# A new written order of operations for attention and token/channel mixing, with one load made to wait for a turned block

## The chip, the cores and the metric

The kernel runs on one core of one Trainium2 chip. The metric is the device time of one execution in microseconds, here the median of three runs. PE is the matmul engine, PEld its weight loads, DVE the vector engine, ACT the scalar engine, POOL is GpSimd, and SP is the engine that only issues DMAs. Names with a q behind them (SPq) are an engine's issuing part.

## The reference, cut to what matters

Sliding-window attention with a linear distance bias gives x; a token mix and a channel mix with residuals follow.

```python
# q, k, v: (8 batches, 8 heads, 576 positions, 64)
scores = 1/sqrt(64) * q @ k.T - slope[h] * |i - j|      # only 0 <= i - j < 128
x = softmax(scores) @ v                                  # -> (8, 576, 512)
h = relu(x.T @ w_tok1) @ w_tok2                          # 576 -> 256 -> 576
u = x + h.T
out = u + relu(u @ w_ch1) @ w_ch2                        # 512 -> 1536 -> 512
```

## The kernel before

Batches are handled in pairs. The 576 positions of a batch are four blocks of 128 and a tail of 64; in a pair the blocks have the numbers 0 to 3 (even batch), 4 to 7 (odd batch) and 8 (both tails). The work of `side(b)` prepares batch b: loads of q, k and v (POOL, L596, from f32 in memory to bf16 on the chip), their turned form `qkT`, scores (PE, L791 and L837), exponentials (ACT, L806), masks (DVE, L816), the product with v (PE, L871), reciprocals and normalisation (L901, L904 on DVE or L909 on ACT), and the token mix (L933 to L976), which writes `ub`, u in bf16 (DVE, L994). u is then turned to `uT`, by PE in the first batches, from batch 3 on by a transposing DMA that SP issues (L1002). From the second pair on SP's DMAs also turn q and k (L743). `main(b)` is the channel mix of batch b: chunks of four wide matmuls (L1491), or in batches 3 to 7 seven half-size products for eight (`unit`, L1391, with differences `tt` of `uT` made on DVE, L1354, copies out of PSUM into `raw` and `ob` buffers by ACT, L1406, or DVE, L1407, and joins on DVE, L1415 and L1417), then the second layer in the same manner (L1668, sums on DVE L1516, results added at L1639), tails (L1534, L1579, L1586), and stores (L1651, L1595) from SP or, for batches 5 and 6, from POOL. While `main(b)` runs on PE, `side(b + 1)` runs between its matmuls.

All of these are operations of a planner, `Plan`. Each has a number, an engine, the operations that it depends on, and buffers in rings. Nothing is chosen when the kernel is built: `ORDER` lists all operations by number (base 36) in one sequence, and each engine runs those that are its own in that sequence. `ELSEWHERE` lists the operations that run on their second engine (ACT for DVE or the reverse), and `PLACES` gives the ring slot of each buffer in the order of first use. So these three tables fix every engine's order, and which earlier buffer's readers an operation waits for. Semaphores between engines follow from them.

POOL issues its loads in that order from one queue; a load waits until its buffer is free, and those behind it wait too. In addition one operation of POOL, `pd`, a copy of four elements of `uT` into an unused corner of `zero` (L1025), holds POOL until batch 4's four blocks of u are turned:

```python
HOLDS = {4: ("v", 3, 0)}
```

SP's queue holds stores, turns of qk and turns of u in the order of the table.

Of the kernel before, what the change touches and what calls it, by code (L numbers as in the profile page):

```python
# [70 lines left out]
class Plan:  # L71
# [60 lines left out]
    def follow(self):  # L132
# [5 lines left out]
        for x in ELSEWHERE.split():  # L138
            o = ops[number(x)]
            o.eng, o.cost, o.emit = o.other  # L140
        line = {e: [o for o in seq if o.eng == e] for e in ("PE", "ACT", "DVE", "POOL", "SP")}
        succ = {o: [] for o in ops}
        left = {o: len(o.deps) for o in ops}
# [16 lines left out]
        at = dict.fromkeys(line, 0)  # L160
# [123 lines left out]
    def emit(self, spin):  # L284
# [20 lines left out]
        for _, _, go in sorted(work, key=lambda w: w[:2]):  # L305
# [37 lines left out]
ORDER = ("h i 4z f j g 52 k d e 0 l 59 7 1 2 8 4v m 3 4 4x n 4w 9 4y o a 55 5 41 50 42 56 43 53 57 44 51 p 58 54 5c q "  # L343
# [44 lines left out]
ELSEWHERE = ("4w 4y 56 5m 63 6i 71 74 82 86 8a a1 a5 b4 b6 c1 c3 ct cz fb fo ft fw gh gj gn gp gr gt gv h7 j0 j2 jk jw ku "  # L388
             "l5 ls lu m0 n8 na of oo op oz qa qd qq qv qy sl t3 t6 th uc uf uh us vd vi vn wv y0 y2 z5 zx 10a 10f 125 12m "
             "12p 130 13n 13q 144 14e 14h 14w 154")  # L390
PLACES = ("000232243674016170016710104526473452324062714260014501022423400510303647106542202567210123732010446005172042"
          "362051274206715214600503123154312004710320646027513140700140215467140010640713055567102605442020611541127230"
          "025262104700230014425051403512010500312141045110243012320140672042576220135742000764034632027316250001410345"
          "032144211356403132100450246021001275130420276110007602714237320407630130523116201136100600423450014031202753"
          "010221310424602240716150473245124022651103414372613403103250016362440743151304001632203241351701025422040305"
          "000654201226422044020117553524030170503214160073144603151242005002361430470201452220764207205106323324401126"
          "21054020440646533020470006402521147105523572030164250114")
UNIT_LATE = False
SECOND_LATE = False
GATE = True  # L400
# [33 lines left out]
def kernel(  # L434
# [15 lines left out]
    nc = tc.nc  # L450
# [464 lines left out]
    def token_mix(b, rank):  # L915
# [13 lines left out]
        for j in range(NJ):  # L929
            turn_ = blocks[1:] + blocks[:1] if half and pr in PAIRED else blocks  # L930
            for c, blk in enumerate(turn_):
                def go(j=j, c=c, blk=blk):
                    pe_.matmul(t1[j]()[:, :], lhsT=W1[:, blk % NC, j * P : (j + 1) * P], rhs=xb()[:, blk, :],  # L933
                               start=c == 0, stop=False)
# [62 lines left out]
        for blk in blocks:  # L997
            if b >= FROM_U:
                def turn(blk=blk):
                    c = blk % NC  # L1000
                    to = uTt()[:, :, :] if blk == TAIL else uT()[:, :, c * P : (c + 1) * P]
                    nc.sync.dma_start_transpose(out=to, in_=ub()[:, blk, :])  # L1002

                turned.setdefault(b, []).append(plan.op(
                    "SP", 1200, turn, rank(0), part=(uTt if blk == TAIL else uT, blk), reads=[(ub, blk)], bus=1000))
                continue
            ut = bank()

# [752 lines left out]
```

## Time and profile before

| | |
|---|---|
| median of 3 runs | 274.56 us (272.98 to 274.78) |
| profiled execution, own time | 274.01 us |
| its span, first to last instruction | 272.1 us |
| busy in the span: PE, DVE, ACT, POOL | 263.2, 234.0, 159.5, 114.8 us |
| instructions of PE, DVE, ACT, POOL | 3033, 533, 306, 147 |
| DMA: moved, packets | 38.59 MB, 160338 |

The span is shorter than the execution's own time by 1.9 us, which lie before the first and behind the last instruction. Busy time of PE is the time in which at least one matmul is in flight; matmuls overlap, so a busy PE can still start them late. A "turn" is a transposing DMA. "Landing" is the time at which a DMA's data are there, "issue" that at which its engine sends it.

### The profile page before, as it was taken

To read this page: it belongs to the slowest core of one execution; us is meant where nothing else is said; L and a number is where in the kernel's file an instruction comes from. 1 tells how busy PE (TensorE), PEld (TensorE's weight loads), DVE (VectorE), ACT (ScalarE), POOL (GpSimd) and SP (SyncE) were. 2 spreads that over 40 slices of the span, in tenths; PEclk is the share of its full clock that TensorE was granted. 3 is DMA by queue.
4 is the path that set the end of the run, shared out by engine and by line. 5 is a ranking of instruction groups with operands and counts; after the bars stand their busy time and mean duration, and the time that the engine had idled before them with its cause. 6 is when DMAs were issued, how large, how long until landed. Compare 5 with 4: busy or idle time off the path is not lost.

```text
span 272.1 us, 7520 instructions
## 1 busy us (share of the span) xinstructions
PE 263.2 (97%) x3033; PEld 195.6 (72%) x3033; DVE 234.0 (86%) x533; ACT 159.5 (59%) x306; POOL 114.8 (42%) x147
## 2 busy tenths in 40 slices
PE   7989999999999999999999999999899989999994
PEld 5767565776686656588877876688776768588883
DVE  7886598983996799889999899999899989987992
ACT  6974787144963469229991299428881379413900
POOL 8987977640680866601680137400740410003000
PEclk9999999999999999999999999999999999999999
DMA  8999999999999999999999899979999430044006
GB/s 197 179 170 181 150 191 183 149 111 181 190 142 169 176 139 230 161 116 232 80 177 149 221 141 78 124 183 164 147 165 111 129 107 2 12 88 149 8 0 193
DMA packets 160338, 38.59 MB, mean 142 GB/s; under 512 B 146544, under 2 KB 159472, under 8 KB 160304
## 3 DMA queue, kind: packets, MB, share of 16 engines
q0 software_dynamic: 109968, 19.64, 90.3%
q1 hardware_dynamic: 49104, 17.70, 33.9%
q10 hardware_dynamic: 1232, 0.79, 1.0%
q8 instruction: 23, 0.38, 0.6%
q14 instruction: 11, 0.09, 0.1%
HBM read 35.85 MB, written 9.44 MB: 166 GB/s over the span
## 4 chain that ended last, share of the span: by engine, by line
PE 71%; DMA 11%; issue 7%; DVE 5%; POOL 4%; ACT 1%; SPq 0%; POOLq 0%; DVEq 0%
PE ps L1668 24%; PE ps L1391 11%; PE ps L1491 11%; PE ps L871 5%; PE ps L933 4%; PE ps L976 4%; PE ps L791 3%; DMA qk<-in_k_dram 3%; PE ps L1534 3%; PE ps L1579 3%; DMA v<-in_v_dram 2%; DMA qkT<-qk 2%; DMA W<-in_moe_w_tok_dram 2%; POOL qk L596 2%; DVE r L1415 2%
## 5 line engine op out<-in xcount | busy, mean ns | idle before, releaser
L806 ACT ACTIVATE pe<-ps 128x1024 bf16<-128x1024 f32 (+1 forms) x56 | 51.8, 971 | 15.8 <-PE ps L791 15.8
L596 POOL DMA_DIRECT2D qk<-in_k_dram x35 | 29.9, 868 | 52.2 <-DMA qkT<-qk 49.0
L596 POOL DMA_DIRECT2D v<-in_v_dram x36 | 30.9, 867 | 30.8 <-PE ps L871 29.9
L1668 PEld LDWEIGHTS <-r 128*128 128x128 bf16 x384 | 36.6, 98 | 8.0 <-issue 1.3
L596 POOL DMA_DIRECT2D qk<-in_q_dram x35 | 30.3, 875 | 11.4 <-DMA qkT<-qk 7.6
L816 DVE TENSOR_TENSOR pe<-pe,mask 128x1024 bf16<-128x1024 bf16 (+1 forms) x48 | 30.3, 647 | 3.4 <-ACT pe L806 3.2
L1491 PE MATMUL ps<-uT,WC 128*128 128x512 bf16 x132 | 32.0, 379 | 0.0
L1406 ACT COPY raw<-ps 128x512 f32<-128x512 f32 x32 | 19.0, 596 | 21.8 <-PE ps L1391 11.9
L1668 PEld LDWEIGHTS <-s 128*128 128x128 bf16 x288 | 27.7, 98 | 5.2 <-issue 0.4
L909 ACT ACTIVATE xb<-ps,rt 128x64 bf16<-128x64 f32 x80 | 18.3, 324 | 19.2 <-DVE rt L901 19.1
L1415 DVE TENSOR_TENSOR r<-ps,raw 128x512 bf16<-128x512 f32 x37 | 24.6, 679 | 1.8 <-PE ps L1391 1.7
L1391 PE MATMUL ps<-tt,WS 128*128 128x256 bf16 x180 | 25.9, 273 | 0.0
L1668 PE MATMUL ps<-WC,r 128*128 128x256 bf16 x192 | 25.7, 273 | 0.0
L1391 PEld LDWEIGHTS <-WS 128*128 128x128 bf16 x240 | 21.9, 98 | 4.9 <-issue 1.2
L871 PEld LDWEIGHTS <-pe 128*128 128x128 bf16 (+1 forms) x480 | 20.4, 99 | 6.5 <-issue 1.4
L1668 PE MATMUL ps<-WT,r 128*128 128x256 bf16 x192 | 24.7, 273 | 0.0
L1668 PE MATMUL ps<-WT,s 128*128 128x256 bf16 x192 | 24.1, 273 | 0.0
L871 PE MATMUL ps<-v,pe 128*128 128x65 bf16 (+1 forms) x480 | 23.0, 194 | 0.6 <-ACT pe L806 0.3
L994 DVE TENSOR_TENSOR ub<-ps,xb 128x512 bf16<-128x512 f32 x32 | 21.0, 683 | 2.9 <-PE ps L976 2.7
L1497 ACT ACTIVATE r<-ps 128x512 bf16<-128x512 f32 x26 | 15.1, 613 | 10.0 <-PE ps L1491 8.7
L1639 DVE TENSOR_TENSOR raw<-ps,ub 128x512 f32<-128x512 f32 x27 | 18.3, 683 | 2.1 <-PE ps L1668 2.1
L1491 PEld LDWEIGHTS <-WC 128*128 128x128 bf16 x132 | 11.6, 98 | 11.8 <-issue 0.2
(145 smaller groups left out, 519.1 us busy)
## 6 DMA issues: line engine op xcount, KB each, us to landing
out_dram<-raw SPq DMA_DIRECT2D x19, 256.0 KB, 2.6
qk<-in_q_dram POOLq DMA_DIRECT2D x30, 128.0 KB, 4.9
qk<-in_k_dram POOLq DMA_DIRECT2D x30, 128.0 KB, 4.9
v<-in_v_dram POOLq DMA_DIRECT2D x28, 128.0 KB, 5.6
WC<-in_moe_w_ch_dram POOLq DMA_DIRECT2D x8, 384.0 KB, 7.6
out_dram<-raw POOLq DMA_DIRECT2D x8, 256.0 KB, 2.8
out_dram<-ob SPq DMA_DIRECT2D x5, 256.0 KB, 2.6
v<-in_v_dram POOLq DMA_DIRECT2D x16, 64.0 KB, 4.8
```

The lines of the kernel that those rows point to most:

```text
L596: nc.gpsimd.dma_start(out=to()[p0 : p0 + n, :, :], in_=rows(src, b, s0, n))
L806: act_.activation(out=pb()[:, e, :, lo:, c0:c1_], in_=wide(e)[:, :, lo:, c0:c1_], func=ACT.Exp, scale=scale)
L816: dve_.tensor_tensor(out=o, in0=o, in1=heads(mk, es), op=ALU.mult)
L871: pe_.matmul(view(e)[a:z, i, :], lhsT=pb()[:, e, i, kind, a:z], rhs=vb()[:, HEADS[e][i], 0 : D + 1], start=start, stop=stop, skip_group_ch ...
L909: act_.activation(out=x4()[:, i, :], in_=view(e)[r0:r1_, i, 0:D], func=ACT.Copy, scale=rt()[r0:r1_, 0, i, :])
L994: plan.op("DVE", 690, lambda blk=blk, ht=ht, hs=hs: dve_.tensor_tensor(out=ub()[:, blk, :], in0=ht()[:, hs], in1=xb()[:, blk, :], op=ALU.a ...
L1391: pe_.matmul(bk()[:, c * HS : (c + 1) * HS], lhsT=l(c, cb), rhs=r(cb), start=new and c == 0 and cb == 0, stop=cb == 1, skip_group_check=True)
L1406: return plan.op("ACT", 600, lambda: act_.copy(out=e()[:, :], in_=bk()[:, :]), rk + UNIT_RANK, makes=e, uses=[bk], other=("DVE", 690, lamb ...
L1415: add = plan.op("DVE", 690, lambda: dve_.tensor_tensor(out=o(), in0=half_of(bk), in1=half_of(e), op=ALU.add), rk + UNIT_RANK, uses=[bk, e] ...
L1491: pe_.matmul(ct()[:, :], lhsT=WC1[:, cb, t * P : (t + 1) * P], rhs=uT()[:, cb, :], start=cb == 0, stop=cb == NCB - 1)
L1639: dve_.tensor_tensor(out=v, in0=bk().rearrange("p (c n) -> p c n", c=2), in1=src, op=ALU.add)
L1668: pe_.matmul(bk()[:, c * HN : (c + 1) * HN], lhsT=l(t, c), rhs=w(t), start=first, stop=g == 1 and t == HK - 1, skip_group_check=True)
```

## The change

`ORDER`, `ELSEWHERE` and `PLACES` are replaced by new tables of the same length and kind: the same 1528 operations, numbered alike, in another sequence, with another choice of engine for part of those that have two, and other buffer slots. From the start, PE, DVE, ACT and POOL keep their order for about 23 us. A new table, `WAITS`, has one entry, `30:pc`: operation `30`, POOL's load of v for block 4 of the third pair (batches 4 and 5), depends on `pc`, SP's turn of block 3 of u of batch 4. In POOL's order the load is preceded by a copy of one element of that block of `uT`.

```diff
         for x in ELSEWHERE.split():
             o = ops[number(x)]
             o.eng, o.cost, o.emit = o.other
+        for x in WAITS.split():
+            o, d = (ops[number(y)] for y in x.split(":"))
+            o.deps.add(d)
+            o.emit = lambda d=d, go=o.emit: (d.touch(), go())
...
-ORDER = ("h i 4z f j g 52 k d e 0 l 59 7 1 2 8 4v m 3 4 4x n 4w 9 4y o a 55 5 41 50 42 56 43 53 57 44 51 p 58 54 5c q "
...
-         "6w 13 6t 73 6r 6x 74 79 6u 14 6y 75 17 6z 76 7g 7a 7b 7h 70 77 7c 78 7d 9k 7i 71 7j 7k 7e 7r 9l 7f 9m 9p 9q "
...
+         "6w 13 6t 73 6r 6x 74 79 6u 14 6y 75 7g 6z 7a 7h 70 76 7b 7i 17 18 77 9k 7j 78 71 7c 9l 7d 9m 7k 9n 7s 7q 1a "
...
+WAITS = "30:pc"
...
+                def touch(blk=blk):
+                    at = 0 if blk == TAIL else blk % NC * P
+                    nc.gpsimd.tensor_copy(out=zero[0:1, 2 * P : 2 * P + 1],
+                                          in_=(uTt() if blk == TAIL else uT())[0:1, 0, at : at + 1])
+
                 turned.setdefault(b, []).append(plan.op(
                     "SP", 1200, turn, rank(0), part=(uTt if blk == TAIL else uT, blk), reads=[(ub, blk)], bus=1000))
+                turned[b][-1].touch = touch
```

Lines behind the insertions move: a line of before stands 5 lines further on behind the tables (L596 is L601), and 11 further on behind the token mix (L1651 is L1662). Three places of the new order follow; rows give line, operation, output and inputs with buffer numbers, and the output's shape.

POOL at the load that now waits, before. The load `30` is the row that writes `v1_73`; loads of `qk` bring q or k of one block, loads of `v` the values.

```order
L596 DMA v3_75<-in_v_dram 128x8x64
L596 DMA qk1_68<-in_q_dram 128x8x64
L596 DMA qk0_67<-in_q_dram 128x8x64
L596 DMA v1_73<-in_v_dram 128x8x64
L596 DMA qk0_67<-in_k_dram 128x8x64
L596 DMA qk3_70<-in_k_dram 128x8x64
L596 DMA qk4_71<-in_q_dram 128x8x64
L596 DMA v0_72<-in_v_dram 128x8x64
```

And POOL after, at the same load, which now writes `v3_75`:

```order
L601 DMA qk4_71<-in_k_dram 128x8x64
L601 DMA qk4_71<-in_q_dram 128x8x64
L601 DMA qk3_70<-in_q_dram 128x8x64
L1011 COPY zero_117<-uT1_99 1x1
L601 DMA v3_75<-in_v_dram 128x8x64
L601 DMA qk3_70<-in_k_dram 128x8x64
L601 DMA qk4_71<-in_q_dram 128x8x64
L601 DMA qk2_69<-in_k_dram 128x8x64
L601 DMA v1_73<-in_v_dram 128x8x64
L601 DMA v4_76<-in_v_dram 128x8x64
L601 DMA qk0_67<-in_k_dram 64x8x64
L1036 COPY zero_117<-uT1_99 1x4
```

The waiting copy stands ahead of the load; the loads of v for blocks 5 and 6 (`v1_73`, `v4_76`) stand behind it. Operation `pd` (the last row) comes 25 rows earlier than before, where it stood among the last stores. Among the turns of batch 4 that of block 3 is now the third of four, where it was the fourth.

SP behind the turns of batch 5's u, before. `uTt0_100` is the tail's turn; the row that writes `qkT0_77` turns the block whose scores PE runs next.

```order
L1002 DMA_TRANSPOSE uT1_99<-ub0_92 128x4x128 x4
L1651 DMA out_0_dram<-raw1_105 128x2x256
L743 DMA_TRANSPOSE qkT2_79<-qk1_68 128x8x128
L1651 DMA out_0_dram<-raw3_107 128x2x256
L743 DMA_TRANSPOSE qkT3_80<-qk2_69 128x8x128
L1002 DMA_TRANSPOSE uTt0_100<-ub0_92 128x4x128
L1651 DMA out_0_dram<-raw0_104 128x2x256
L743 DMA_TRANSPOSE qkT4_81<-qk3_70 128x8x128
L1651 DMA out_0_dram<-raw4_108 128x2x256
L743 DMA_TRANSPOSE qkT0_77<-qk0_67 128x8x128
```

SP after, at the same place; the same turn now writes `qkT1_78`:

```order
L1007 DMA_TRANSPOSE uT0_98<-ub1_93 128x4x128 x4
L748 DMA_TRANSPOSE qkT6_83<-qk3_70 128x8x128
L1662 DMA out_0_dram<-raw1_105 128x2x256
L1007 DMA_TRANSPOSE uTt0_100<-ub1_93 128x4x128
L748 DMA_TRANSPOSE qkT5_82<-qk1_68 128x8x128
L748 DMA_TRANSPOSE qkT1_78<-qk2_69 128x8x128
L1662 DMA out_0_dram<-ob0_109 128x2x256
L1662 DMA out_0_dram<-raw0_104 128x2x256
L1662 DMA out_0_dram<-raw3_107 128x2x256
L748 DMA_TRANSPOSE qkT4_81<-qk4_71 128x8x128
L748 DMA_TRANSPOSE qkT6_83<-qk0_67 128x8x128
```

That turn now stands ahead of three stores; of the other turns of this stretch one has gone far ahead, and two stand behind the stores.

POOL's stores of batch 5, before; `ob0_109` is the tail's result, in two halves.

```order
L1595 DMA out_0_dram<-ob0_109 64x512
L1651 DMA out_0_dram<-raw4_108 128x2x256
L1651 DMA out_0_dram<-raw0_104 128x2x256
L1595 DMA out_0_dram<-ob0_109 64x512
L1651 DMA out_0_dram<-raw2_106 128x2x256
L1025 COPY zero_117<-uT0_98 1x4
L1651 DMA out_0_dram<-raw3_107 128x2x256
```

After:

```order
L1606 DMA out_0_dram<-ob0_109 64x512 x2
L1662 DMA out_0_dram<-raw2_106 128x2x256
L1662 DMA out_0_dram<-raw0_104 128x2x256 x2
L1662 DMA out_0_dram<-raw4_108 128x2x256
L1662 DMA out_0_dram<-raw1_105 128x2x256
```

Both halves of the tail now go first. The copy of the product that PE waited behind (L1407 on DVE before, into `raw0_104`) runs on ACT after (into `raw2_106`), and the store that frees its buffer is the third one of the row in both.

More of the change, by code (lines that the diff above doesn't have):

```diff
@@ L345 @@
          "x 6v 5u 5r y 6j 5s 46 47 66 72 6k 5v z 6a 48 6b 10 6d 6l 6g 6e 6h 6f 67 6m 6c 68 6i 11 69 6n 6p 6o 12 6s 6q "
[42 rows of a table removed]
[L388 to L397, printed above, removed]
[42 rows of a table added]
+ELSEWHERE = ("4w 4y 56 5m 63 6i 71 74 78 7b 7f 84 86 88 ai b9 bz c1 c3 cd cj ct cx el fm ft gh gj gp gv gx hf jc ji jl ko "
+             "la ls n8 na oh op oz po pt qa qq qv qy sl t3 t6 u7 uc us vd vi vl wt y2 z8 zg zx 10f 10i 125 12p 13q 13v 140 "
+             "146 149 14b 14e 14h 154")
+PLACES = ("000122344672036170016710104526473452324062734260014501032423100140213475607220046272034001536024216272520001"
+          "067415233720651324602562032157301122443136002107460120531521315331011275000234004217304224465300240402164571"
+          "026203502273020350410523114514224041131020203041251251320240160240617542020615142061257243603201543101720214"
+          "405253711443150312004572021062027502027060276002721420673206540140710020232170022060032410473304456011053421"
+          "401341210462433124070326473012241152642201132213042746022301410106254025121703752003416504460221514200515144"
+          "750204201730416223110204006532135065132470316020131004031240452060540521120100471220761572205306322750021132"
+          "64100210704650611734500306212410753404174012530615235213")
+WAITS = "30:pc"
 UNIT_LATE = False
```

82 rows, old and new, of the table ORDER are left out of this document.

## The prediction

> **What bounds the kernel now.** First the page's part on busy time and its row of the granted clock.
>
> ```profile
> span 272.1 us, 7520 instructions
> PE 263.2 (97%) x3033; PEld 195.6 (72%) x3033; DVE 234.0 (86%) x533; ACT 159.5 (59%) x306; POOL 114.8 (42%) x147
> PEclk9999999999999999999999999999999999999999
> ```
>
> PE is busy for 263.2 of 272.1 us, at full clock throughout, and the change neither adds nor removes a matmul. So what it can win is idle time of PE, 272.1 - 263.2 = 8.9 us, and what it can cost is new idle time. The second view, PE's waits, says which idle time that is (releaser, us in total, times, longest).
>
> ```profile
> PE ps L1726 <- DVE zero L547: 1.0, 1, 1.0
> PE ps L1391 <- DVE raw L1407: 0.9, 1, 0.9
> PE ps L791 <- DMA qkT<-qk: 0.7, 1, 0.7
> PE ps L1209 <- ACT pe L1103: 0.5, 1, 0.5
> PE ps L1232 <- DMA W<-in_moe_w_tok_dram: 0.5, 1, 0.5
> PE ps L754 <- DMA qk<-in_k_dram: 0.3, 1, 0.3
> PE ps L871 <- ACT pe L806: 0.3, 1, 0.3
> PE ps L1726 <- ACT qkT L1055: 0.3, 1, 0.3
> PE ps L871 <- DVE xb L904: 0.2, 1, 0.2
> PE ps L1078 <- DVE slant L564: 0.2, 1, 0.2
> ```
>
> Five of them (L1726 twice, L1209, L1232, L1078; 2.5 us) belong to the opening: PE's order is the same in both kernels for its first 43 planned operations, up to 22.9 us. At the other end the chain of waits has its last PE piece at 267.14 us; 267.14 + 1.32 = 268.46, and 3.6 us of add and store follow, which both kernels have.
>
> ```profile
> 267.14 1.32 PE ps L1579 x12
> ```
>
> What is left are five waits, 2.4 us in sum. The timeline gives their places (start, us, in brackets the idle time before), and what each costs in truth.
>
> ```profile
> 28.93 0.40 PE L754 MATMUL ps<-ident,qk 128*128 128x128 bf16 x4 [0.35 <-DMA qk<-in_k_dram]
> 163.12 0.40 PE L871 MATMUL ps<-v,pe 128*128 128x65 bf16 x8 [0.26 <-ACT pe L806]
> 165.45 0.40 PE L871 MATMUL ps<-v,pe 128*128 128x65 bf16 x8 [0.25 <-DVE xb L904]
> 191.22 0.41 PE L871 MATMUL ps<-v,pe 128*128 128x65 bf16 x8
> 192.36 0.23 PE L791 MATMUL ps<-qkT 64*128 64x128 bf16 x2 [0.73 <-DMA qkT<-qk]
> 220.03 0.69 DVE L1407 COPY raw<-ps 128x512 f32<-128x512 f32 x1 [1.03 <-DMA out_dram<-raw]
> ```
>
> A printed gap is shorter than the loss, because the matmul before it has a tail that a successor would have overlapped. The row ahead of the gap at 192.36 us spans 191.22 to 191.63 with eight matmuls; if the last of them takes about 0.2 us, it starts near 191.43, and the next work could have begun at about 191.47: 0.89 us lost where 0.73 is printed. I add this 0.16 to each of the five: 0.35, 0.26, 0.25, 0.73 and 0.90 become 0.51, 0.42, 0.41, 0.89 and 1.06, together **3.3 us, or 1.2%**. That is all that a new order can win behind the opening, as far as this trace shows. (1% is about what a measurement of this kernel can tell from no change.)
>
> **The change part by part.**
>
> *The wait.* Load `30` of POOL (v of batch 5, block 4) gets one more instruction, a copy of one element that waits for the turn of u's block 3 of batch 4. The nearest row is the copy of four elements that is there already, 0.18 us.
>
> ```profile
> 217.65 0.18 POOL L1025 COPY zero<-uT 1x4 bf16<-1x4 bf16 x1
> 127.95 0.88 POOL L596 DMA_DIRECT2D v<-in_v_dram  x1 [14.37 <-PE ps L871]
> 141.99 0.88 POOL L596 DMA_DIRECT2D qk<-in_q_dram  x1 [0.17 <-issue]
> 143.39 5.54 SPq L1002 DMA_TRANSPOSE uT<-ub  x4
> 155.15 0.87 POOL L596 DMA_DIRECT2D qk<-in_k_dram  x1 [12.28 <-DMA qkT<-qk]
> 158.63 0.42 PE L871 MATMUL ps<-v,pe 128*128 128x65 bf16 x8
> ```
>
> Before, POOL resumes at 127.95, issues loads up to 142.87, SP sends the four turns of batch 4 from 143.39 to 148.93, and POOL then stands for 12.28 us behind a buffer of qk. After, eleven loads go ahead of the wait; at 0.88 each that is 9.7 us, so POOL reaches it near 138 and stands there until the turn lands, some 11 us. One stand takes the place of another, and PE pays nothing for the stand or for the 0.18 us as such. But behind the waiting load stand three loads of q and k and then v of block 5, which the value matmuls at 158.63 need together with load 30. Is that in time? Before, all four turns are sent by 148.93; after, that of block 3 goes third instead of fourth, so at 143.39 + 2 x 1.4 = 146.2 if the four slots are even. From issue to landing the trace has, for turns of u (shortest, median, longest) and for loads (median, the last number):
>
> ```profile
> DMA to landing us min/median/max: 2.3/3.0/4.6
> qk<-in_q_dram POOLq DMA_DIRECT2D x30, 128.0 KB, 4.9
> v<-in_v_dram POOLq DMA_DIRECT2D x28, 128.0 KB, 5.6
> ```
>
> With no load in flight I take 2.6 for the turn, between the shortest and the median: landed at 148.8. Then 0.3 for the copy, four issues of 0.88 (3.5), and 5.6 for the fifth load: **158.2**. PE asks for it at 158.63, less the 0.5 won at 28.9: 158.1. By the medians that is a tie. The bounds: turn 2.3 and load 4.9 give 157.2, no stall; turn 4.6 and load 5.6 give 160.2, 2.1 us of stall. I take no stall, nearer to the lower end, because the medians come from loads and turns mixed, while here the DMA engines have emptied when the burst starts.
>
> What does the wait win? Before, loads land beside these turns, and DVE waits for the last of them:
>
> ```profile
> L1354 DVE TENSOR_TENSOR tt<-uT 128x512 bf16<-128x512 bf16 x1 | 0.4, 426 | 0.7 <-DMA uT<-ub 0.7
> ```
>
> PE has no wait at that place in its list: second-product matmuls lie over DVE's 0.7 us. So I count 0.
>
> *SP's order at 185 to 192 us.* Two turns of qk are sent between stores of batch 4, one takes 5.9 us, and PE waits for the second.
>
> ```profile
> 185.41 1.29 SPq L743 DMA_TRANSPOSE qkT<-qk  x1
> 186.80 0.54 SPq L1651 DMA_DIRECT2D out_dram<-raw  x1
> 187.43 1.76 SPq L743 DMA_TRANSPOSE qkT<-qk  x1
> 185.41 5.90 DMA qkT<-qk
> DMA to landing us min/median/max: 3.1/3.6/8.3
> ```
>
> Between the last wide turn of batch 5's u and the turn that PE waited for stood four stores, three turns of qk and the tail's turn; now it is one store, two turns of qk and the tail's. It moves up by 3 x 0.54 + 1.29 = 2.9 us, against a loss of 0.89, which I count as gone. What is late next is the turn that now goes last, behind three stores: its reader is the score group after next, about 3 us further on. No gap is counted for it, and the allowance for new gaps below covers it.
>
> *POOL's stores at 212 to 220 us.* A copy out of PSUM on DVE (L1407) waited 1.03 us for the buffer of the third store, and PE behind it. After, the copy for the same product runs on ACT and takes the buffer of the third store again, with the same add ahead of the first store. The bounds are 0 and 1.06; nothing favours either end, so I take half, 0.53.
>
> *The gap at 28.9 us.* A four-matmul chunk of L1491 (eight take 1.73 us, so 0.86) now goes ahead of the transposes that lost 0.51, and POOL's two loads for them keep their places. It is gone.
>
> *163 to 166 us.* Here PE waits for ACT's exponentials and DVE's normalisation. The change moves work between the two:
>
> ```profile
> L909 ACT ACTIVATE xb<-ps,rt 128x64 bf16<-128x64 f32 x80 | 18.3, 324 | 19.2 <-DVE rt L901 19.1
> L904 DVE TENSOR_TENSOR xb<-ps,rt 128x256 bf16<-128x256 f32 (+1 forms) x44 | 17.7, 416 | 0.5
> L1417 DVE TENSOR_SCALAR r<-r 128x512 bf16<-128x512 bf16 x24 | 8.0, 349 | 0.1
> ```
>
> Six normalisations net go from ACT (four instructions each) to DVE: 6 x 0.416 = 2.5 us more on DVE. Eight relus and copies net go from DVE to ACT, at 0.35 (L1417) to 0.69 (the copy above): 2.8 to 5.5 us less. Over 234 us of DVE that is next to nothing, so it decides only locally; of 0.42 + 0.41 I take half, 0.42.
>
> *New gaps.* Behind 23 us every engine's order is new, with DVE at 86%. Before has five gaps in 245 us; I allow one of about their middle size: 0.5.
>
> **The sum:** 0.51 + 0.89 + 0.53 + 0.42 - 0.5 = 1.85 us won. The profiled execution took 274.01 us for its span of 272.1; 274.01 - 1.85 = 272.2. The median of before, 274.56, lies 0.55 above that execution: **272.7 us**.
>
> **Rivals.**
>
> - *All five gaps go and no new one comes:* 3.3 us, 271.3. For it: two of the five are DMA waits that the order takes up directly. Against: DVE and ACT stay as full as they were. 0.27.
> - *PE has more room than its gaps show.* If the share of its weight loader, 72%, were its true load, 28% of 272.1, 76 us, would be room, and an order that found a tenth of it would end near 267. Against it:
>
> ```profile
> 62.24 1.73 PE ps L1491 x8
> L1491 PEld LDWEIGHTS <-WC 128*128 128x128 bf16 x132 | 11.6, 98 | 11.8 <-issue 0.2
> ```
>
>   Here a matmul starts every 216 ns without a pause and its loader works for 98 of them, 45%: a low share is the width of the matmul. 0.02. [...]
> - *The wait binds.* If the turn of block 3 lands later than 148.7, v of block 5 lands behind 158.1 by the medians, and each load behind it is as late. Price 2.1 us at the slow end; with the gains of the other edits undone by the late loads behind, 274.56 + 2.1 = 276.7, and near 278 if the burst also holds up the qk turn that SP sends beside it (turns of u spread from 2.3 to 4.6, those of qk up to 8.3). For it: the tie. Against: DMA engines without loads for ten microseconds. 0.12. [...]
> - *Nothing moves:* the gaps change places, 274 to 275.2. For it: PE at 97%, the stores' chain as before. 0.14.
> - *The wait is empty,* since the turn has landed when POOL gets there. Not so by the times above: POOL near 138, the turn issued near 146.
>
> **How the numbers follow.** Forecast 0.45 (271.8 to 274), all gaps gone 0.27, more room 0.02, nothing moves 0.14, the wait binds 0.12 (0.08 of it above 277.3, 1% over the median). Faster by over 1% (below 271.8) 0.29, slower by over 1% 0.08, within 0.63. The range goes from 270.5, the price of all gaps less 5 x 0.16 for tails twice as long as I took them, to 276.4, just short of the binding wait; that leaves out some 0.15.
>
> **What would show it.** Right: PE's waits without the qk turn near 191 and the k load near 29; near 218 a wait for a raw buffer of under 1 us; a stand of POOL of some 11 us that ends with a turn of u near 149. Wrong: value matmuls waiting for a load of v near 158, or a qk turn waited for behind 150. I would also be wrong if loads of the second layer's weights, some of which move behind loads of batch 2, came late for L1668 near 49 us.

## The result and the profile after

| | before | after |
|---|---|---|
| median of 21 runs | 274.46 us (272.51 to 276.45) | 272.57 us (270.90 to 274.14) |
| profiled execution, own time | 274.01 us | 272.57 us |
| its span | 272.1 us | 270.8 us |

The ratio is 0.9935, 95% interval 0.9911 to 0.9959: 1.8 us, a real gain, and under 1%. Medians here and below are of all runs, while ratios leave out the slow ones, those over 1.5% above the fastest of the same kernel, so a ratio need not be the quotient of two medians (furthest off is `a_waitfirst`: 1.0069, where the medians give 1.0115). The forecast was 272.7 us. The number is right. The experiments show that two steps of its sum are wrong and cancel: the wait, counted at nothing, is worth some 2.8 to 4.6 us, and the new tables without it, counted as a gain, make the kernel slower. That the total came out is luck.

The page of after, span and busy time:

```profile
span 270.8 us, 7505 instructions
...
PE 262.5 (97%) x3033; PEld 195.0 (72%) x3033; DVE 231.1 (85%) x531; ACT 158.9 (59%) x290; POOL 115.4 (43%) x148
```

PE is as full as before (97% of the span in both). Its list of waits (releaser, us in total, times, longest):

```profile
PE ps L1402 <- DMA uT<-ub: 1.2, 1, 1.2
PE ps L1737 <- DVE zero L552: 1.0, 1, 1.0
PE ps L1063 <- DVE qk L634: 0.8, 1, 0.8
PE ps L1220 <- ACT pe L1114: 0.5, 1, 0.5
PE ps L1737 <- ACT qkT L1066: 0.3, 1, 0.3
PE ps L1089 <- DVE slant L569: 0.2, 1, 0.2
PE ps L1402 <- ACT pe L811: 0.2, 1, 0.2
```

Of the five waits behind the opening four are gone: the k load at 28.9 us, the normalisation at 165, the qk turn at 192, the copy behind a store at 219. The exponential near 163 still costs a little. New is the first row, 1.2 us for the turns of batch 4, the very turns of the new wait. The timeline shows the place: PE, then POOL and SP (start, us, in brackets the idle time before).

```profile
149.54 1.47 PE L1679 MATMUL ps<-WT,r 128*128 128x256 bf16 x12
152.24 0.61 PE L1402 MATMUL ps<-uT,WC 128*128 128x256 bf16 x4 [1.23 <-DMA uT<-ub]
...
153.23 0.82 PE L1679 MATMUL ps<-WC,s 128*128 128x256 bf16 x6
...
154.75 0.82 PE L1679 MATMUL ps<-WT,r 128*128 128x256 bf16 x6
```

```profile
144.21 5.37 SPq L1007 DMA_TRANSPOSE uT<-ub  x4
...
149.42 0.44 POOL L1011 COPY zero<-uT 1x1 bf16<-1x1 bf16 x1 [13.58 <-DMA uT<-ub]
149.91 0.90 POOL L601 DMA_DIRECT2D v<-in_v_dram  x1
```

POOL stands 13.6 us, until the third turn has landed; then its burst of loads starts at 149.91, while the fourth turn (sent from 148.35) is on its way. In before PE came to the same product at 152.83, with three groups of the second layer just ahead of it:

```profile
151.52 0.82 PE L1668 MATMUL ps<-WT,r 128*128 128x256 bf16 x6
152.17 0.82 PE L1668 MATMUL ps<-WC,s 128*128 128x256 bf16 x6
152.83 0.60 PE L1391 MATMUL ps<-uT,WC 128*128 128x256 bf16 x4
```

After, two such groups (153.23 and 154.75) stand behind it, so PE asks for the turns at about 150.9 instead of 152.8. Each sign that the prediction named for being right was seen, and none of those for being wrong: this wait was on neither list.

### The profile page after: what moved, and what is told of

Its sections match the earlier page's. It is cut to its first block, busy times and chain, and to the rows that moved or that the text cites. A ratio compares the mean times of both kernels' runs of the same rounds, so it can differ in the third digit from the quotient of the medians.

```text
span 270.8 us, 7505 instructions
## 1 busy us (share of the span) xinstructions
PE 262.5 (97%) x3033; PEld 195.0 (72%) x3033; DVE 231.1 (85%) x531; ACT 158.9 (59%) x290; POOL 115.4 (43%) x148
## 4 chain that ended last, share of the span: by engine, by line
PE 84%; DMA 6%; ACT 5%; DVE 2%; issue 1%; POOL 0%; DVEq 0%; POOLq 0%; ACTq 0%
PE ps L1679 26%; PE ps L1402 14%; PE ps L1502 11%; PE ps L876 5%; PE ps L796 5%; PE ps L938 5%; PE ps L981 5%; PE ps L1545 4%; PE ps L1590 3%; DMA v<-in_v_dram 2%; DMA W<-in_moe_w_tok_dram 2%; ACT pe L811 2%; DMA uT<-ub 1%; PE ps L1488 1%; ACT raw L1417 1%
## 5 line engine op out<-in xcount | busy, mean ns | idle before, releaser
L601 POOL DMA_DIRECT2D v<-in_v_dram x36 | 30.9, 866 | 38.0 <-PE ps L876 36.8
L601 POOL DMA_DIRECT2D qk<-in_k_dram x35 | 30.4, 877 | 22.8 <-DMA qkT<-qk 21.9
L601 POOL DMA_DIRECT2D qk<-in_q_dram x35 | 30.5, 880 | 17.9 <-DMA qkT<-qk 17.0
L1417 ACT COPY raw<-ps 128x512 f32<-128x512 f32 x37 | 21.4, 600 | 26.2 <-PE ps L1402 22.8
L1426 DVE TENSOR_TENSOR r<-ps,raw 128x512 bf16<-128x512 f32 x41 | 27.6, 685 | 3.1 <-PE ps L1402 2.0
L1679 PE MATMUL ps<-WC,r 128*128 128x256 bf16 x192 | 24.8, 273 | 0.0
L876 PEld LDWEIGHTS <-pe 128*128 128x128 bf16 (+1 forms) x480 | 19.4, 99 | 5.6 <-issue 0.8
L914 ACT ACTIVATE xb<-ps,rt 128x64 bf16<-128x64 f32 (+1 forms) x56 | 13.0, 329 | 14.2 <-DVE rt L906 14.1
L909 DVE TENSOR_TENSOR xb<-ps,rt 128x256 bf16<-128x256 f32 (+1 forms) x50 | 20.4, 418 | 0.5
L1502 PEld LDWEIGHTS <-WC 128*128 128x128 bf16 x132 | 11.8, 98 | 12.1 <-DVE uT L1028 0.4
L1402 PEld LDWEIGHTS <-WC 128*128 128x128 bf16 x180 | 16.8, 98 | 4.9 <-DMA uT<-ub 1.7
```

Source lines behind the costliest of these rows:

```text
L601: nc.gpsimd.dma_start(out=to()[p0 : p0 + n, :, :], in_=rows(src, b, s0, n))
L876: pe_.matmul(view(e)[a:z, i, :], lhsT=pb()[:, e, i, kind, a:z], rhs=vb()[:, HEADS[e][i], 0 : D + 1], start=start, stop=stop, skip_group_ch ...
L909: dve_.tensor_tensor(out=x4(), in0=view(e)[r0:r1_, :, 0:D], in1=rt()[r0:r1_, 0, :, :].broadcast_to([r1_ - r0, 4, D]), op=ALU.mult)
L1402: pe_.matmul(bk()[:, c * HS : (c + 1) * HS], lhsT=l(c, cb), rhs=r(cb), start=new and c == 0 and cb == 0, stop=cb == 1, skip_group_check=True)
L1417: return plan.op("ACT", 600, lambda: act_.copy(out=e()[:, :], in_=bk()[:, :]), rk + UNIT_RANK, makes=e, uses=[bk], other=("DVE", 690, lamb ...
L1426: add = plan.op("DVE", 690, lambda: dve_.tensor_tensor(out=o(), in0=half_of(bk), in1=half_of(e), op=ALU.add), rk + UNIT_RANK, uses=[bk, e] ...
```

## The experiments

The theory of the prediction, A: the wait is worth nothing, the gains come from the order. The rival that the result suggests, D (called B in the first run): loads in flight make turns late, so the wait is what makes this order pay. C: the wait itself does harm, because it ends one turn too early. Ratios are to the kernel before, run on the same chip beside them (three chips, before at 274.12, 273.14 and 273.50 us); a difference of under about 0.3% between two kernels is not resolved.

| kernel | last turn of batch 4, issue to landing | PE's wait for it | median, us | ratio (95%) |
|---|---|---|---|---|
| changed kernel, second time (`c_after`) | 3.8 us | 1.04 | 272.66 | 0.9953 (0.9931 to 0.9976) |
| no wait (`a_nowait`) | 5.1 | 2.3 | 276.87 | 1.0103 (1.0068 to 1.0138) |
| wait on a turn long landed (`a_emptywait`) | 5.3 | 2.9 | 275.19 | 1.0055 (1.0026 to 1.0084) |
| wait on the first turn (`a_waitfirst`) | 6.2 | 2.9 | 276.29 | 1.0069 (1.0033 to 1.0105) |
| wait on the last turn (`a_waitlast`) | at most 2.8 | none | 272.13 | 0.9940 (0.9911 to 0.9969) |

The first row is a control, the changed kernel unedited:

> The changed kernel itself, beside the three others on one chip: ratio to before as in the result, 0.9935 within 0.003.

### Without the wait

```diff
-WAITS = "30:pc"
+WAITS = ""
```

> The changed kernel with its wait list empty: load 30 no longer waits for the turn of u's block 3; every order stays. In the changed kernel GpSimd stood 13.6 us ahead of load 30 (135.8 to 149.4), the turns of batch 4 landed at 146.8, 148.1, 149.4 and 152.2 us, and TensorE waited 1.2 us for them (start to start 1.5). Theory A (the prediction: the wait is worth nothing, the gap comes from what SyncE has ahead of the turns): the gap at 150.7 stays between 0.9 and 1.5 us, and the time is that of the changed kernel within 0.5 us, 272.6. Theory B (the wait keeps loads away from the turns): the turns take 2 to 3.4 us from the end of their issue to landing, as in the kernel before, instead of 1.15; the last lands near 153 to 154, the gap grows to 2 to 3 us, time 273.4 to 274.6. Theory C (the wait harms, since the loads that it lets go run into the last turn): the last turn lands near 150.8, the gap is under 0.3 us, time 271.4.

276.87 us: slower than before by 1.0%, and than the changed kernel by more than theory B gave. Batch 4's turns took, from issue to landing:

```profile
DMA to landing us min/median/max: 2.4/3.7/5.1
```

PE's waits in that stretch, and POOL in the timeline:

```profile
PE ps L1402 <- DMA uT<-ub: 2.3, 1, 2.3
```

```profile
138.17 0.88 POOL L601 DMA_DIRECT2D qk<-in_k_dram  x1
149.66 0.88 POOL L601 DMA_DIRECT2D qk<-in_q_dram  x1 [10.61 <-DMA qkT<-qk]
150.52 0.88 POOL L601 DMA_DIRECT2D qk<-in_k_dram  x1
```

POOL stands all the same, at the load two places further on, whose buffer a qk turn has to free. It is let go at 149.66, when the last turn of u has only begun to be sent (149.74). So the burst falls on it, and it takes 5.1 us. The table by microsecond (PE busy, granted clock, DMA share, GB/s) shows a second cost, which no theory had:

```profile
155.00:156.00 1.00, 1.00 (x9) 0.90 2.14 159
156.00:157.00 1.00, 1.00 (x6) 0.50 1.09 80
157.00:158.00 1.00, 1.00 (x6) 0.50 2.44 185
158.00:159.00 1.00, 1.00 (x7) 0.50 2.87 154
159.00:160.00 1.00, 1.00 (x13) 0.89 0.78 233
```

Behind PE's idle time the granted clock halves for 3.4 us, which costs 0.10 + 3 x 0.50 + 0.11 = 1.7 us. Eight of this kernel's nine timed runs had a mean clock of 0.988 to 0.994; of the changed kernel's 21 runs in the result none was under 0.996. Theory A falls, and C as far as it has the wait cost time on the whole.

### The same copy, with nothing to wait for

```diff
-WAITS = "30:pc"
+WAITS = "30:k8"
```

> The changed kernel with the same extra copy ahead of load 30, on a turn of batch 3 (k8) that landed near 121 us: the instruction stays, the waiting goes. Control for the kernel without the wait (276.9 us). Theory D (the wait wins because it keeps the burst of loads 3j, 3h, 33, 36 away from batch 4's turns): as without the wait, GpSimd goes on at 136 us and stands later at load 3j, TensorE waits 2 us or more for the last turn, and the time is 276 to 277.5. Theory E (the kernel without the wait was slow through something else, such as its changed instruction stream or the chip that day): time 272.2 to 273.2, as the changed kernel.

275.19 us: far from E, and on D's side, but under the 276 that D gave at the least. The instruction and its place are those of the changed kernel; only the waiting is gone. The turns of batch 4 again, from issue to landing:

```profile
DMA to landing us min/median/max: 2.4/3.7/5.3
```

PE's wait, and PE in one of the microseconds behind it:

```profile
PE ps L1402 <- DMA uT<-ub: 2.9, 1, 2.9
```

```profile
156.00:157.00 1.00, 1.00 (x11) 1.00 1.62 286
```

Here PE idled even longer, 2.9 us, and in the profiled run the clock did not fall. It fell in 5 of the 12 timed runs: those at a mean clock of 0.988 to 0.994 took 275.1 to 279.4 us, the seven at 0.996 to 1.000 took 274.3 to 275.7.

### The wait on the first turn, and on the last

```diff
-WAITS = "30:pc"
+WAITS = "30:p9"      # a_waitfirst
+WAITS = "30:pa"      # a_waitlast
```

> The changed kernel with the wait on the turn that SyncE sends first (block 0, landed at 146.8 us) in place of the third: the burst is let go near 146.9, with three turns still to land. Theory D (each turn with loads beside it lands 1.5 to 2.7 us later): the last turn lands near 153 to 154.5, TensorE's gap is 2 to 3 us, between the kernel with the wait on the third (1.4) and none (2.5), and the time 273.5 to 276.5, the more the oftener the clock falls. Theory A (the wait is worth nothing): 272.6.

> The changed kernel with the wait on the turn that SyncE sends last (block 1) in place of the third (block 3). Theory C (the load let go at 149.4 us delays the last turn, sent until 149.57, from 1.15 to 2.6 us): the last turn lands near 150.8, the gap of 1.2 us at 150.7 goes. But load 30 and those behind it go 1.3 us later, so v of block 5 lands near 159.1 where TensorE would ask for it near 158.1: a new wait of up to 1.0 us there; time 271.5 to 272.5. Theory A (the last turn is late for another reason): it still lands near 152.2, the gap stays 1.2, the loads go 2.8 us later than in the changed kernel and the value matmuls wait 1.3 us: time near 274.

On the first turn, the burst starts at 146.5, and the last of the three turns behind takes 6.2 us (turns of batch 4, then PE's wait):

```profile
DMA to landing us min/median/max: 2.4/3.1/6.2
```

```profile
PE ps L1402 <- DMA uT<-ub: 2.9, 1, 2.9
```

It costs as much as no wait: 1.0069, with 8 of 12 runs at a clock of 0.988 to 0.994. PE's idle time was within the range expected, though longer than without any wait, not between the two. On the last turn, all four land within 2.8 us, and the 1.2 us at 150.7 are gone; a new wait of 0.4 us comes at 158.6 (the same two views).

```profile
DMA to landing us min/median/max: 2.3/2.4/2.8
```

```profile
PE ps L876 <- DVE r L1426: 0.4, 1, 0.4
```

272.13 us lies in the range that C gave, but 0.9940 can't be told from the changed kernel's 0.9935 and 0.9953. That the burst let go by the third turn makes the fourth late is shown; a gain in time from waiting for the fourth is not.

### PE kept busy through the gap

This is `a_nowait` with ten 128x512 matmuls on zeros ahead of the product that waits (`pi`):

```diff
+        o = self.ops[int("pi", 36)]
+        work.append((o.t0, -1, lambda: spin(banks.slots[[b for b in o.bufs if b.ring is banks][0].slot[0]], 10, 0)))
         for _, _, go in sorted(work, key=lambda w: w[:2]):
             go()
```

> The changed kernel without the wait, and with ten 128x512 matmuls on zeros (216 ns each, 2.2 us) on TensorE ahead of the product that waits for the turns: the turns land as late as without the wait, but TensorE doesn't idle. In the kernel without the wait it idled 2.3 us and then ran at a granted clock of 0.50 from 156 to 159.3 us. Theory F (the idle time itself lowers the clock, which costs 3.3 x 0.5 = 1.65 us beside the gap): the clock stays at 1.00 around 155 to 160 and the time falls from 276.9 to 275.2. Rival (the clock falls for another reason, or it costs nothing): the time stays at 276.9 or more.

PE in the timeline:

```profile
150.95 2.32 PE L1739 MATMUL ps<-zero 128*128 128x512 bf16 x10
153.17 0.61 PE L1404 MATMUL ps<-uT,WC 128*128 128x256 bf16 x4
```

The turns are as late as before (5.0 us), PE doesn't idle, and none of the 12 runs has a clock under 0.998. 274.66 us, ratio 1.0047 (1.0021 to 1.0073): 0.56% under `a_nowait`, as expected. Beside `a_emptywait`, on the same chip, it is 0.5 us, which is not resolved. So at this place the clock fell in 8 of 9 runs with the idle time and in none of 12 with it filled, and where it fell, in the profile of `a_nowait`, that cost 1.7 us. Most of what the wait is worth remains, and that is the gap.

### The turns earlier

The lists can be edited one operation at a time by a few lines that move operation a behind (`a>b`) or ahead (`a<b`) of b, slots unchanged:

```diff
+        asked = list(seq)
+        for x in MOVES.split():
+            o, d = (ops[number(y)] for y in x.replace("<", ">").split(">"))
+            seq.remove(o)
+            seq.insert(seq.index(d) + (">" in x), o)
...
+MOVES = "ru>pa i4>ru i0>i4"
```

> The changed kernel with one qk turn (ru) and two stores (i0, i4), which SyncE sends ahead of batch 4's turns of u from 141.2 to 144.2 us, moved behind them; the wait stays. u's blocks are written at 142.0, 143.5, 145.2 and 146.4 us, so the turns can go from 142.1 to 147.7 instead of 144.2 to 149.6. Theory A (the gap at 150.7 is SyncE's list): the last turn lands by 150.4, the gap is under 0.2 us, GpSimd is let go near 146.7 instead of 149.4, and the time is 1.2 us below the changed kernel's, 271.4. Rival (the gap moves): the turn ru, now sent near 149, lands behind 154.2, where scores of block 5 read it, or the burst of loads collides with the two last turns; then the gap is given back there and the time is 272.6 within 0.4.

274.21 us, ratio 1.0031 (0.9996 to 1.0066). The turns landed in 2.3 to 2.4 us each, sent from 142.3 on, and the gap at 150.7 is gone. It came back behind 158.8 (the turns of batch 4, PE's longest wait, and ACT in the timeline):

```profile
DMA to landing us min/median/max: 2.3/2.4/2.4
```

```profile
PE ps L887 <- ACT raw L1428: 1.4, 1, 1.4
```

```profile
154.58 1.07 ACT L1428 COPY raw<-ps 128x512 f32<-128x512 f32 x2 [2.21 <-DMA out_dram<-raw]
```

One of the two stores that I moved (`i4`) held the buffer into which ACT was to copy from 152.4 on, and ACT stood 2.2 us for it. Of its 12 timed runs four had a clock of 0.988 to 0.994. That is the rival, at a place that I hadn't named, and dearer: it gave the time of the changed kernel, 272.6.

### Cover put back

Cover is work that PE can do while the turns are on their way. The changed kernel with the two groups that it had taken from ahead of the product, or their like, put back:

```diff
+MOVES = "mr<pi n1<pi"
```

> The changed kernel, wait on the third turn as it is, with two products of the second unit (mr, n1; 0.65 us each), which stand on TensorE behind the first product that reads the turns of batch 4 (pi), moved ahead of it. In the kernel before, TensorE came to pi at 152.83 us with two more products ahead of it (mu, mr) than in the changed kernel, which was ready for it at 150.86. Theory G (the changed order took the cover of the turns away, by 1.3 us): the gap at 150.7 shrinks from 1.4 us to 0.1 to 0.3, and the time falls by up to 1.1 us, to 0.990 of before. Rival (the two products were cover for DVE's work a little later): a new wait of 0.5 us or more between 153 and 158, and the time stays at 0.9935.

PE's only wait between 140 and 160 us is now another, behind a DVE sum at 158.05 (timeline of PE):

```profile
152.73 0.60 PE L1413 MATMUL ps<-uT,WC 128*128 128x256 bf16 x4
...
158.05 0.23 PE L807 MATMUL ps<-qkT 64*128 64x128 bf16 x2 [0.36 <-DVE raw L1661]
```

So G explains the new gap: 1.3 us of cover removed it. The time did not follow: 272.29 us, 0.9953 (0.9937 to 0.9969), that of the changed kernel on the same chip, as the rival had it, with a new wait smaller than its 0.5.

### Three of the gaps of before, taken out by one move each

```diff
+MOVES = "9r>85 xe<x2 wa<w6"
```

> The kernel before with three of its gaps taken out by one move each and nothing else: the transposes at 28.9 us (9r) go behind the next product (85), the qk turn that TensorE waited for at 192 us (xe) goes ahead of another qk turn (x2) on SyncE, and the store whose buffer DVE waited for at 219 us (wa) goes ahead of the one in front of it (w6) on GpSimd. Theory A (each gap is worth its start-to-start loss on the whole): 0.51 + 0.89 + 1.06 = 2.46 us less than before, ratio 0.991, and TensorE's list of waits has none of the three. Theory B (the work behind the gaps is bound by others, so the time comes back as new waits behind them): the three waits go, but TensorE's list shows others of 0.5 us and more behind 30 us, and the time falls by less than 1.5 us. By the prediction's half for the third, 1.93.

275.49 us, ratio 1.0056 (1.0027 to 1.0085): slower. The three waits are gone, and others are there (PE's waits, then PE and SP in the timeline, then SP in before):

```profile
PE ps L1545 <- DMA uTt<-ub: 1.5, 1, 1.5
...
PE ps L1402 <- ACT raw L1417: 0.7, 1, 0.7
```

```profile
29.41 0.99 PE L1737 MATMUL ps<-zero 128*128 128x512 bf16 x9
...
184.68 1.22 SPq L1013 DMA_TRANSPOSE uTt<-ub  x1
```

```profile
183.45 1.23 SPq L1002 DMA_TRANSPOSE uTt<-ub  x1
```

The qk turn moved up pushed the tail's turn down SP's queue, from 183.45 to 184.68, and PE waited 1.5 us for that, more than the 0.9 to be won. At 219 the copy on DVE no longer waits, but PE waits 0.7 for one on ACT. At 29 the planner put nine matmuls on zeros, 1.0 us, where it reckoned with a gap, so that this third of the experiment says nothing about the move. B is right, and the time even rose: a gap is worth its length only if what comes next is ready too.

### Trying for a better version

```diff
-WAITS = "30:pc"
+WAITS = "30:pa"             # a_best1
+MOVES = "x2>pa"             # a_best1, a_best2
+WAITS = "30:pa 2s:k8"       # a_best2
```

> The changed kernel with the wait on the last turn (block 1), and with a qk turn that is read only at 189 us (x2) moved from ahead of batch 4's turns on SyncE to behind them. With the wait on the last turn alone the gap at 150.7 went, but value matmuls waited 0.4 us (0.67 start to start) at 158.6 for work behind the loads let go 1.5 us later. SyncE spends 1.4 us on x2 and waits for its loads, so the turns should land 1.3 us earlier, by 149.6, and load 30 go as early as in the changed kernel (149.4). Theory D: neither gap, time 271.2 to 271.8, ratio to before 0.990. Rival: u's blocks, written until 146.4 us, hold the turns; then nothing is won over the wait on the last turn, 272.1.

> The changed kernel with the wait on the last turn of batch 4, the qk turn x2 behind batch 4's turns, and a second wait of the same kind one batch earlier: load 2s, with 2u and 34 behind it, waits for the turn of u that is sent last but one in batch 3 (k8). With the first two alone the only wait left between 25 and 160 us was one of 0.8 us (1.07 start to start) for batch 3's turns at 120.7. Theory D (loads in flight delay turns wherever they meet): the turns of batch 3 land 1 to 2 us earlier, the wait at 121 goes, and the time falls by a further 0.4 to 1.0 us, ratio near 0.989. Rival (the loads that wait are late for SyncE's qk turns at 124 to 127 us): SyncE and with it the turns behind are late, TensorE waits for a qk turn near 132, ratio 0.994 or more.

`a_best1`: 271.68 us, ratio 0.9936 (0.9908 to 0.9963). `a_best2`: 272.12 us, 0.9945 (0.9925 to 0.9964), beside the changed kernel's 0.9953 on the same chip. Of PE's waits D was right: between 25 and 160 us the first has one left, at 121 for batch 3's turns (0.8 us); the second, with a wait for those as well, has none for a turn, but a new one of 0.4 us on DVE near 135. The rows of the two:

```profile
PE ps L1413 <- DMA uT<-ub: 0.8, 1, 0.8
```

```profile
PE ps L887 <- DVE rt L917: 0.4, 1, 0.4
```

The ratios that D gave, 0.990 and 0.989, were not reached, and neither is shown to beat the changed kernel.

### The wait's work done by order

```diff
-WAITS = "30:pc"
+WAITS = ""
+MOVES = "33>30 36>33 ru>pa"
```

> The changed kernel without the wait, the same end sought by order alone: the two loads of v that stood behind the burst (33, 36) go directly behind load 30, so at 137 to 140 us, and the qk turn whose buffer load 3j needs (ru) goes behind batch 4's turns, so that the burst 3j, 3h can't start before them. Theory D (what counts is that no load runs beside the last turns, not the wait as such): the last turn lands 1.1 to 2 us after its issue, by 150.5, the gap at 150.7 is under 0.5 us, and the ratio is 0.990 to 0.994. Rival (the four early loads still run beside the first turns, and the qk turn comes late for the scores that read it near 154): gap or new wait over 1 us, ratio 0.997 to 1.006.

274.03 us, ratio 1.0034 (1.0010 to 1.0058): not what D expected of it. The four loads that now go at 137 to 141 us take 4.9 us to landing by the medians of their kinds, so by that the last of them reaches into the time of the turns, sent from 144.2 on; the turns take 3.1 to 6.6 us (turns of batch 4, then PE in the timeline):

```profile
DMA to landing us min/median/max: 3.1/4.9/6.6
```

```profile
153.09 0.60 PE L1413 MATMUL ps<-uT,WC 128*128 128x256 bf16 x4
```

The last landed near 152.4, where D gave 150.5: DVE waited 0.4 us for the turns, until 152.42. PE shows no wait for them, but in this run it came to the product late, at 153.09, having lost 1.5 us in the opening (last section), so the profile can't tell whether they would have been in time, and where the rest of the time goes is open. What is shown is that these two moves do not replace the wait.

## Why the number was right and two of its terms were not

By the rule of the prediction (printed gap and 0.16 us of tail, an estimate there; the rows of before at 151.52, 152.17 and 152.83, with no gap between them, overlap by 0.17 and 0.16), from the two lists of waits and the rows above and below; 0.38 is what remains near 163, the row under the table:

| term | forecast, us | measured, us |
|---|---|---|
| 28.9, k load | 0.51 | 0.51 |
| 163 to 166 | 0.42 | 0.83 - 0.38 = 0.45 |
| 192, qk turn | 0.89 | 0.89 |
| 219, copy behind a store | 0.53 | 1.06 |
| new gaps | -0.5 | -1.39 |
| opening (the same matmuls start at 22.46 and 22.50) | 0 | -0.04 |
| sum | 1.85 | 1.48; the two executions differ by 1.44 |

The waits in the opening add up to 2.5 us before and 2.8 after, but PE leaves it at the same time.

```profile
163.87 0.60 PE L1402 MATMUL ps<-uT,WC 128*128 128x256 bf16 x4 [0.22 <-ACT pe L811]
```

- **The gaps named.** All four terms came as forecast or better. For 219 I had only bounds and took half. What happened: POOL began its stores 1.3 us earlier, they landed in 2.5 to 2.7 us instead of 2.9 to 4.4, and the copy, now on ACT, waits for PE only (timeline of after):

```profile
212.95 1.12 POOL L1606 DMA_DIRECT2D out_dram<-ob  x2 [10.44 <-DVE ob L1597]
217.40 1.07 ACT L1417 COPY raw<-ps 128x512 f32<-128x512 f32 x2 [0.41 <-PE ps L1402]
```

- **The wait, counted 0: the step that failed.** It read "PE has no wait at that place in its list: second-product matmuls lie over DVE's 0.7 us", which holds for the order of before (no run puts the wait into that order). The order of after has two of those groups behind the product (`a_cover`), so PE stands where only DVE stood. In that order a burst of loads on the turns costs PE 2.3 to 2.9 us and often the clock besides (a mean of 0.988 to 0.994 in 8 of 9, 5 of 12 and 8 of 12 runs of `a_nowait`, `a_emptywait` and `a_waitfirst`). The wait's worth is the changed kernel against the same without it: 1.0055 - 0.9953 = 1.0%, 2.8 us, by the control with the empty wait, and 1.0103 - 0.9935 = 1.7%, 4.6 us, at the most, each with an interval of about 0.4% to both sides. The profiles agree with the lower value: without the wait PE waits 2.3 - 1.2 = 1.1 us longer for the turns and the clock costs 1.7, together 2.8; with the empty wait 2.9 - 1.2 = 1.7, and the clock's 1.7 in 5 of 12 runs, 2.4 on the mean. The spans of `a_nowait` and the changed kernel differ by 4.3 (275.1 and 270.8), but 0.9 of that lies in the opening, which the wait can't touch (the same matmuls start at 23.37 and 22.50), and 0.4 in a wait for the turns of batch 3 at 122 us that the changed kernel's profile lacks.
- **The order, counted at +1.85, is by itself a loss**: 0.55% to 1.03%, 1.5 to 2.8 us, although four of the five gaps that I had listed are gone in its profiles too. The 2.9 us won there are spent on the turns of batch 4 (2.3 and the tail, 2.45) and on the clock (1.7). Order here means the three tables together, which no run takes apart. -1.5 + 2.8, or -2.8 + 4.6, gives the 1.3 to 1.8 that was measured, but that is no second proof, since both terms are differences to the same runs.
- **The new gap.** The allowance of 0.5 stood for gaps unknown. One came, 1.39, at a place that the sum had looked at and called covered. It is not worth its length, though: taken away in three ways (`a_waitlast`, `a_cover`, `a_best1`), it left the time within 0.3%, with smaller waits behind it.
- **POOL's stand** was forecast at 11 us with an end at 149; it was 13.6, with an end at 149.4. The tie at 158 was in time: PE has no wait for a load of v there. The rival "the wait binds" was not seen in any run, that with the wait on the last turn included.
- **The other rivals.** "All five gaps go" failed by the new gap. "Nothing moves" is excluded by the interval. With an empty wait (`a_emptywait`) the kernel is slower than before.
- **The burst and the turns.** A turn of batch 4 took 2.3 to 2.4 us from issue to landing in `a_turnsfirst`, where POOL stood while they were sent, and the slowest one 5.0 to 6.2 where the burst fell on it (`a_nowait_fill` 5.0, `a_nowait` 5.1, `a_emptywait` 5.3, `a_waitfirst` 6.2). With the wait on the third turn three of four are out of reach of the burst, and the fourth takes 3.8; with the wait on the last all four are, at 2.8 us at the most.

## What to carry to other kernels

When an order is replaced, look up what stands ahead of each waiting instruction in the new order, not only whether it waited in the old; cover that is moved away turns a neutral transfer into the bound (here 1.3 us of it, for a wait of 1.2 us). A wait added to a load queue can protect a transfer that other engines wait for: here it kept the burst off three turns or all four, by the turn that released it, though between those two no difference in time is shown. Judge an edit that has two parts by running each alone, since a right total says nothing about its terms.

## What the runs showed of the hardware that was not expected

- Idle time of PE of 2.3 us was followed by half the granted clock for 3.4 us in one profile (`a_nowait`, 0.50 from 156 to 159 us), and 2.9 us of idle by none in two others (`a_emptywait` and `a_waitfirst`, 1.00 in every microsecond from 149 to 162). A mean clock of 0.988 to 0.994 was seen in 8 of 9, 5 of 12 and 8 of 12 timed runs of these three, and in 0 of 12 where matmuls on zeros filled the gap; with the changed kernel's 1.0 to 1.2 us of idle, in 0 of 21 and 1 of 12. But it was also seen in 4 of 12 in `a_turnsfirst`, with 1.4 us of idle in its profile, and in 2 of 12 and 1 of 12 in `a_byorder` and `a_waitlast`, whose profiles have none there; how long PE idled in the runs that weren't profiled isn't known. How much idle time brings the clock down is not shown.
- The opening, in which PE's order is the same, differs by up to 2.0 us between profiles. In that of `a_byorder` (first fence) PE's 11 small matmuls on zeros took 1.35 us where `c_after` (second) has 0.79, and the same scores start at 16.45 and 14.93, at a granted clock of 1.00 in both records up to 25 us; ACT's exponential nearest to them (L1215, L1204) starts at 16.71 and 15.19, and in `a_waitfirst` at 14.69. Why is open.

```profile
8.76 1.35 PE L1748 MATMUL ps<-zero 128*128 128x128 bf16 x11
...
16.45 0.33 PE L1117 MATMUL ps<-qkT 64*128 64x128 bf16 x6
```

```profile
7.78 0.79 PE L1737 MATMUL ps<-zero 128*128 128x128 bf16 x11
...
14.93 0.33 PE L1106 MATMUL ps<-qkT 64*128 64x128 bf16 x6
```
